# Later transposes by crossbar DMA, weights loaded behind them, PSUM banks given out by what was freed first, last output tile in two halves

## Chip, cores and metric

One core of one Trainium2 chip runs the whole program. The metric is the device time of one execution in microseconds; the lower the better. Executions of the kernel before lie within 0.6% of each other (238.12 to 239.59 us over all rounds), so a few tenths of a microsecond count only when the median of several runs, or the stage lengths of the traces, show them. "Span" is the part of an execution that the profile covers; the time of an execution is longer than its span by about two microseconds.

## The reference

A parallel transformer block in bf16: layernorm without weights, then sliding-window attention and a gated feed-forward, both from the same normalised rows, both added to the input.

```python
x: [1, 2048, 448]          # S = 2048, D = 448
xn = (x - mean) / sqrt(var + 1e-5)
q, k, v = split(xn @ wqkv) # H = 16 heads of Dh = 28
p  = softmax(mask(q @ k.T * Dh**-0.5))      # causal, window W = 256
a  = (p @ v) @ wo
b  = (gelu_tanh(xn @ w_gate) * (xn @ w_up)) @ w_down   # F = 1792
out = x + a + b
```

## The kernel before

It works in four blocks of 512 rows. Each block has an attention stage (twelve steps: four head groups of three steps, each with scores, an exponential on ScalarE, masks on GpSimd; after each group the product PV of the masked exponentials with V) and a gated feed-forward stage. While ScalarE computes exponentials, TensorE gets other work as filler: the down projection of the block before (`gen_down`) and the projections of the block after (`gen_proj`). The kernel uses eight PSUM banks; four hold the scores, the other four go by tags: `m` (two rotating), `d` and `o` (one each).

```python
    def transp(t, n, copy, tag):          # rows -> columns, on TensorE
        tp = psum.tile([P, 2, 4, P], bf16, name="tp", tag=tag, bufs=2 if tag == "m" else 1)
        for i in range(n):
            xn = xns.pop(t + i)
            for c in range(4):
                nc.tensor.transpose(out=tp[:, i, c, :], in_=xn[:, c, :], identity=ident[:, :])
        copy(out=xnT[:, :, t * P:(t + n) * P].rearrange("p c (i q) -> p i c q", q=P), in_=tp[:, 0:n, :, :])

    def gen_proj(qb):
        for t in (4 * qb, 4 * qb + 2):
            tag = ring[0][ring[1] % len(ring[0])]
            ring[1] += 1
            transp(t, 2, nc.vector.tensor_copy, tag)
            yield -830                    # nominal ns of filler
        yield from gen_v(qb, (4 * qb, 4 * qb + 2))
        yield from gen_qk(qb, range(4))

    def gen_down(qb, tags="odod"):        # one output tile of 128 rows at a time
        for tt in range(4):
            down_tag[0] = tags[tt]
            po = psum.tile([P, QB], f32, name="po", tag=tags[tt], ...)
            # 4 matmuls with wo, 14 with wd, yielding after every two        (cut)
            res = work.tile([P, D], bf16, name="res")
            nc.vector.tensor_tensor(out=res[:, :], in0=po[:, 0:D], in1=x_sb[:, t, :], op=ALU.add)
            nc.sync.dma_start(out=outv[:, t, :], in_=res[:, :])

    # gated(): up banks alternate between both m and both single ones
        turn = [0, 1] * 4
        # ... in begin(f)                                                 (cut)
            if f not in early:
                for tag, n in ((("m", 2), ("m", 2)), (("d", 1), ("o", 1)))[turn.pop(0)]:
                    pr["us"].append(psum.tile([P, QB], f32, name="u0", tag=tag, bufs=n))

    # attention(): PV takes the single bank that the current output tile does not hold
            ov = psum.tile([P, QB], f32, name="ov", tag="d" if down_tag[0] == "o" else "o", bufs=1)
```

## Time and profile before

| | before |
|---|---|
| time, median | 238.4 us (238.29 to 238.52; over all later rounds 238.12 to 239.59) |
| span of the profiled execution | 237.3 us (time of that execution 239.04) |
| first matmul of the V projection | 7.74 us |
| attention stages 1, 2, 3 (first `po` to first `u`) | 32.47, 32.51, 31.18 us |
| gated stages 1, 2, 3 (first `u` to first `po`) | 22.77, 22.77, 15.92 us |
| last addition starts | 231.73 us |

### The profile page before, as it was taken

To read this page: it belongs to the slowest core of one execution; us is meant where nothing else is said; L and a number is where in the kernel's file an instruction comes from. 1 tells how busy PE (TensorE), PEld (TensorE's weight loads), DVE (VectorE), ACT (ScalarE), POOL (GpSimd) and SP (SyncE) were. 2 spreads that over 40 slices of the span, in tenths; PEclk is the share of its full clock that TensorE was granted. 3 is DMA by queue.
4 is the path that set the end of the run, shared out by engine and by line. 5 is a ranking of instruction groups with operands and counts; after the bars stand their busy time and mean duration, and the time that the engine had idled before them with its cause. 6 is when DMAs were issued, how large, how long until landed. Compare 5 with 4: busy or idle time off the path is not lost.

```text
span 237.3 us, 4191 instructions
## 1 busy us (share of the span) xinstructions
PE 224.2 (94%) x1716; PEld 95.4 (40%) x1716; DVE 139.6 (59%) x283; ACT 135.2 (57%) x115; POOL 93.4 (39%) x116
## 2 busy tenths in 40 slices
PE   7799999999999999999999999999999899999990
PEld 2434333344544434344444434444344344333450
DVE  6897887769636666656634686464421865486211
ACT  4577798434967866322877768233587678363000
POOL 5024677220256877010075776220055867420000
PEclk9999999999999999999999999999999999999997
DMA  6999900000000000000000000000000000000010
GB/s 223 353 326 312 267 5 0 0 3 1 0 22 0 23 19 19 3 0 1 0 22 0 22 0 22 19 0 3 0 0 22 19 0 22 19 3 0 23 40 29
DMA packets 9010, 10.95 MB, mean 46 GB/s; under 512 B 600, under 2 KB 7960, under 8 KB 8984
## 3 DMA queue, kind: packets, MB, share of 16 engines
q1 hardware_dynamic: 8440, 9.81, 13.3%
q10 hardware_dynamic: 544, 0.80, 1.0%
q8 instruction: 15, 0.25, 0.5%
q14 instruction: 11, 0.09, 0.1%
HBM read 8.77 MB, written 1.84 MB: 45 GB/s over the span
## 4 chain that ended last, share of the span: by engine, by line
PE 78%; ACT 10%; DVE 4%; DMA 3%; issue 1%; POOL 1%; SPq 0%; ACTq 0%
PE gt L203 16%; PE po L288 16%; PE u L203 9%; ACT p_sb L450 7%; PE sc L446 6%; PE gt L208 5%; PE ov L420 4%; PE pq L203 4%; PE pk L203 4%; PE ue L203 4%; PE pv L203 3%; PE po L283 3%; DMA wv<-in_A_wqkv_dram 3%; PE pq L208 2%; ACT ge L357 2%; ACT L577 1%
## 5 line engine op out<-in xcount | busy, mean ns | idle before, releaser
L456 POOL TENSOR_SCALAR_AFFINE_SELECT p_sb<-p_sb 128x512 bf16<-128x512 bf16 (+1 forms) x92 | 69.6, 778 | 93.6 <-ACT p_sb L450 93.5
L450 ACT ACTIVATE p_sb<-sc 128x2048 bf16<-128x2048 f32 (+2 forms) x48 | 85.0, 1771 | 24.8 <-PE sc L446 20.6
L357 ACT ACTIVATE ge<-gt 128x1024 bf16<-128x1024 f32 x28 | 28.7, 1024 | 47.1 <-PE u L208 24.6
L288 PE MATMUL po<-wd,hT 128*128 128x448 bf16 x224 | 50.1, 353 | 0.0
L203 PE MATMUL gt<-xnT,wg 128*128 128x512 bf16 x168 | 40.5, 380 | 0.0
L361 DVE TENSOR_TENSOR hT<-ge,u 128x512 bf16<-128x512 bf16 x42 | 26.9, 683 | 18.4 <-ACT ge L357 18.3
L203 PE MATMUL u<-xnT,wu 128*128 128x512 bf16 x126 | 30.6, 379 | 0.6 <-DVE hT L322 0.6
L411 POOL TENSOR_TENSOR oN<-oc,rb 128x512 bf16<-128x512 f32 x16 | 21.0, 1314 | 23.8 <-DVE rb L405 23.8
L288 PEld LDWEIGHTS <-hT 128*128 128x128 bf16 x224 | 20.1, 98 | 20.5 <-issue 4.0
L424 DVE COPY oc<-ov 128x512 f32<-128x512 f32 x16 | 11.0, 690 | 22.2 <-PE ov L420 20.8
L203 PEld LDWEIGHTS <-wg 128*128 128x128 bf16 x168 | 15.1, 98 | 22.1 <-issue 6.0
L203 PEld LDWEIGHTS <-wu 128*128 128x128 bf16 x168 | 15.9, 98 | 20.0 <-issue 2.0
L446 PE MATMUL sc<-qT,kT 32*128 32x128 bf16 (+2 forms) x352 | 18.5, 275 | 1.6 <-ACT p_sb L450 1.1
L283 PE MATMUL po<-wo,oN 128*128 128x448 bf16 x64 | 15.9, 353 | 0.5 <-DVE hT L361 0.5
L293 DVE TENSOR_TENSOR res<-po,x_sb 128x448 bf16<-128x448 f32 x16 | 9.9, 616 | 10.1 <-PE po L288 10.0
L322 DVE CAST hT<-ue 128x512 bf16<-128x512 f32 x14 | 9.0, 683 | 11.1 <-PE ue L208 11.1
L420 PE MATMUL ov<-p_sb,v_sb 128*32 128x128 bf16 (+2 forms) x352 | 12.8, 277 | 1.5 <-POOL oN L411 0.8
L203 PE MATMUL pq<-xnT,wqp 128*128 128x512 bf16 (+1 forms) x51 | 13.3, 368 | 0.3 <-DVE v_sb L234 0.3
L208 PE MATMUL gt<-xnT,wgu 64*128 64x512 bf16 x49 | 13.3, 379 | 0.0
L203 PE MATMUL pk<-xnT,wkp 128*128 128x512 bf16 (+1 forms) x51 | 13.1, 366 | 0.1
L203 PE MATMUL pv<-wv,xnT 128*128 128x448 bf16 x48 | 11.1, 354 | 1.7 <-DMA wv<-in_A_wqkv_dram 1.4
L252 DVE CAST kT<-pk 128x512 bf16<-128x512 f32 (+1 forms) x17 | 10.9, 643 | 2.5 <-PE pk L208 2.5
(67 smaller groups left out, 206.0 us busy)
## 6 DMA issues: line engine op xcount, KB each, us to landing
out_dram<-res SPq DMA_DIRECT2D x16, 112.0 KB, 1.7
wd<-in_B_w_down_dram SPq DMA_DIRECT2D x1, 1568.0 KB, 12.8
wu<-in_B_w_up_dram SPq DMA_DIRECT2D x1, 1344.0 KB
wg<-in_B_w_gate_dram SPq DMA_DIRECT2D x1, 1344.0 KB, 14.5
x_sb<-in_A_x_dram SPq DMA_DIRECT2D x1, 896.0 KB
wraw<-in_A_wqkv_dram ACTq DMA_DIRECT2D x1, 672.0 KB
x_sb<-in_A_x_dram SPq DMA_DIRECT2D x1, 448.0 KB
wo<-in_A_wo_dram SPq DMA_DIRECT2D x4, 98.0 KB
```

The costliest lines, as they stand in the source:

```text
L203: nc.tensor.matmul(ps, lhsT=lhs(c), rhs=rhs(c), start=start and c == 0, stop=stop and c == 2, skip_group_check=True)
L208: nc.tensor.matmul(ps, lhsT=lhs[p0:p0 + 64], rhs=rhs[p0:p0 + 64], start=start, stop=stop, tile_position=(p0, 0), skip_group_check=True)
L283: nc.tensor.matmul(po[:, 0:D], lhsT=oN[:, g, cs], rhs=wo[:, g, :], start=(g == 0), stop=False, skip_group_check=True)
L288: nc.tensor.matmul(po[:, 0:D], lhsT=hT[:, f, cs], rhs=wd[:, f, :], start=False, stop=(f == NF - 1), skip_group_check=True)
L357: nc.scalar.activation(out=ge[:, :, :], in_=pr["gt"][:, :, :], func=ACT.Gelu_apprx_tanh)
L361: nc.vector.tensor_tensor(out=hT[:, f + i, :], in0=ge[:, i, :], in1=u[:, :], op=ALU.mult)
L411: nc.gpsimd.tensor_tensor(out=oN[:, g, :], in0=oc[:, :], in1=rb[:, :, :].rearrange("p a b -> p (a b)"), op=ALU.mult)
L420: nc.tensor.matmul(ov[32 * j:32 * j + 32, q0:q0 + nq], lhsT=v_sb[:, kt, h, :], rhs=p_sb[:, j, col:col + nq], start=(n == 0 and i == 0), st ...
L424: nc.vector.tensor_copy(out=oc[:, :], in_=ov[:, :])
L446: nc.tensor.matmul(ss[:, j, col:col + nq], lhsT=kT[r, g, kt * P:(kt + 1) * P], rhs=qT[r, g, qb * QB + q0:qb * QB + q0 + nq], start=True, s ...
L450: nc.scalar.activation(out=p_sb[:, :, 0:ncol], in_=ss[:, :, 0:ncol], func=ACT.Exp, scale=SCALE)
L456: nc.gpsimd.affine_select(out=reg, in_=reg, pattern=mid + [[1 if diag else -1, P]], compare_op=ALU.is_ge, fill=0.0, base=0 if diag else -1 ...
```

## The change

Four things, all to take TensorE work or TensorE waits away. (1) Tiles 4 to 15 are transposed by crossbar DMA (`dma_start_transpose`, a transfer that writes the tile transposed), and the weights, which would stand ahead of them in the same queue, are issued behind the first four (`loads`, called once tiles 6 and 7 are normalised in block 0). (2) The banks for up projections, output tiles and PV are chosen with the aim that the one freed first is used first. (3) In blocks 1 and 2 one pair of up projections moves from the gated stage into attention as filler, and the filler is shared out differently (`late`, `fresh`). (4) The last output tile is computed, added and stored in two halves.

```diff
+    def dma_transp(t):
+        nc.sync.dma_start_transpose(out=xnT[:, :, t * P:(t + 1) * P], in_=xns.pop(t)[:, :, :].rearrange("p a b -> p (a b)"))
 ...
     def gen_proj(qb):
-        for t in (4 * qb, 4 * qb + 2):
-            tag = ring[0][ring[1] % len(ring[0])]
-            ring[1] += 1
-            transp(t, 2, nc.vector.tensor_copy, tag)
-            yield -830
 ...
-    def gen_down(qb, tags="odod"):
+    def gen_down(qb, tags):
+            for n, (lo, up) in enumerate(((0, D),) if t < NT - 1 else ((0, D // 2), (D // 2, D))):
+                    if g % 2:
+                        fresh[0] = g == 1
 ...
-        turn = [0, 1] * 4
+        turn = [down_tag[0], "o" if down_tag[0] == "d" else "d"] * 4
 ...
+                alone = (turn.pop(0), 1)
+                tags = (("m", 2), alone)
+                if qb == 0 and f == 0:
+                    nxt = [ring[0][(ring[1] + i) % 3] for i in range(2)]
 ...
-                    share(feeds, whole / (left + 0.2) - ahead - to, to)
+                    late = 400 if i == 0 else 0
+                    share(feeds, (whole - late) / (left + 0.2) + late - ahead - to, to)
+                    if n == 0 and g and fresh[0]:
+                        feeds[0].run()
 ...
+    def loads():
+        for t in range(4, 8):
+            dma_transp(t)
+        nc.sync.dma_start(out=wu[:, :, :], in_=rows(B_w_up, 0, 3))
+        # ... the half rows, wg, wo, wd                                   (cut)
 ...
-            feeds = [Feed((gen_down(qb - 1), DOWN))]
+            tags = "dodo" if last_tag[0] == "o" else "odod"
+            feeds = [Feed((gen_down(qb - 1, tags), DOWN))]
-                plan = {0: 830, 1: 830, 2: 1140, 4: 1140, 5: 1300, 7: 1300, 8: 1300, 10: 1300}
+                new_hT(qb)
+                early = (2,)
+                feeds[1].gens.append(gen_up(qb, early))
+                feeds[1].left += UP1
+                plan = {0: 1140, 2: 1140, 4: 1300, 5: 1300, 7: 1300, 8: 1300, 10: 1300}
 ...
-    feed = Feed((gen_down(NB - 1, "dmom"), DOWN))
+    feed = Feed((gen_down(NB - 1, "dmomd" if last_tag[0] == "o" else "omdmo"), DOWN))
```

More of the change, by code (lines that the diff above doesn't have):

```diff
@@ L139 @@
     nc.sync.dma_start(out=x_sb[:, 8:16, :], in_=xv[:, 8:16, :])
-    nc.sync.dma_start(out=wu[:, :, :], in_=rows(B_w_up, 0, 3))
-    for t3, lo, hi in ((wgu3, B_w_gate, B_w_up), (wug3, B_w_up, B_w_gate)):
-        nc.sync.dma_start(out=t3[0:64, :], in_=lo[384:448, :])
-        nc.sync.dma_start(out=t3[64:128, :], in_=hi[384:448, :])
-    nc.sync.dma_start(out=wg[:, :, :], in_=rows(B_w_gate, 0, 3))
     eps_t = const.tile([P, 1], f32, name="eps_t")
@@ L257, in gen_proj @@
     def gen_proj(qb):
-        for t in (4 * qb, 4 * qb + 2):
-            tag = ring[0][ring[1] % len(ring[0])]
-            ring[1] += 1
-            transp(t, 2, nc.vector.tensor_copy, tag)
-            yield -830
         yield from gen_v(qb, (4 * qb, 4 * qb + 2))
         yield from gen_qk(qb, range(4))
-    PROJ, QK1 = 2 * 830 + 2 * 1500 + 4 * 1660, 1660
+    PROJ, QK1 = 2 * 1500 + 4 * 1660, 1660
     DOWN = 4 * 3400
@@ L271 @@
     hTs, oNs = {}, {}
-    down_tag = ["d"]
-    def gen_down(qb, tags="odod"):
+    down_tag, last_tag, fresh = ["d"], [None], [False]
+    def gen_down(qb, tags):
         hT, oN = hTs[qb], oNs[qb]
@@ L279, in gen_down @@
             cs = slice(tt * P, (tt + 1) * P)
-            down_tag[0] = tags[tt]
-            po = psum.tile([P, QB], f32, name="po", tag=tags[tt], bufs=2 if tags[tt] == "m" else 1)
-            for g in range(4):
-                nc.tensor.matmul(po[:, 0:D], lhsT=oN[:, g, cs], rhs=wo[:, g, :], start=(g == 0), stop=False,
-                                 skip_group_check=True)
-                if g % 2:
-                    yield 380
-            for f in range(NF):
-                nc.tensor.matmul(po[:, 0:D], lhsT=hT[:, f, cs], rhs=wd[:, f, :], start=False, stop=(f == NF - 1),
-                                 skip_group_check=True)
-                if f % 2 and f < NF - 1:
-                    yield 375
-            res = work.tile([P, D], bf16, name="res")
-            nc.vector.tensor_tensor(out=res[:, :], in0=po[:, 0:D], in1=x_sb[:, t, :], op=ALU.add)
-            nc.sync.dma_start(out=outv[:, t, :], in_=res[:, :])
-            yield 375
+            for n, (lo, up) in enumerate(((0, D),) if t < NT - 1 else ((0, D // 2), (D // 2, D))):
+                w = up - lo
+                tag = tags[tt + n]
+                down_tag[0] = tag
+                po = psum.tile([P, QB], f32, name="po", tag=tag, bufs=2 if tag == "m" else 1)
+                for g in range(4):
+                    nc.tensor.matmul(po[:, 0:w], lhsT=oN[:, g, cs], rhs=wo[:, g, lo:up], start=(g == 0), stop=False,
+                                     skip_group_check=True)
+                    if g % 2:
+                        fresh[0] = g == 1
+                        yield 380 * w // D
+                fresh[0] = False
+                for f in range(NF):
+                    nc.tensor.matmul(po[:, 0:w], lhsT=hT[:, f, cs], rhs=wd[:, f, lo:up], start=False, stop=(f == NF - 1),
+                                     skip_group_check=True)
+                    if f % 2 and f < NF - 1:
+                        yield 375 * w // D
+                res = work.tile([P, D], bf16, name="res")
+                nc.vector.tensor_tensor(out=res[:, 0:w], in0=po[:, 0:w], in1=x_sb[:, t, lo:up], op=ALU.add)
+                nc.sync.dma_start(out=outv[:, t, lo:up], in_=res[:, 0:w])
+                yield 375 * w // D
     def new_hT(qb):
@@ L328, in gated @@
         hT = hTs[qb]
-        turn = [0, 1] * 4
+        turn = [down_tag[0], "o" if down_tag[0] == "d" else "d"] * 4
         def begin(f):
+            last_tag[0] = turn[0] if f not in early else last_tag[0]
             pr = dict(f=f, gt=phase[0].pool.tile([P, 2, QB], f32, name="gt", tag="s"), us=[])
             if f not in early:
-                for tag, n in ((("m", 2), ("m", 2)), (("d", 1), ("o", 1)))[turn.pop(0)]:
+                alone = (turn.pop(0), 1)
+                tags = (("m", 2), alone)
+                if qb == 0 and f == 0:
+                    nxt = [ring[0][(ring[1] + i) % 3] for i in range(2)]
+                    tags = [(x, 2 if x == "m" else 1) for x in nxt]
+                for tag, n in tags:
                     pr["us"].append(psum.tile([P, QB], f32, name="u0", tag=tag, bufs=n))
@@ L529 @@
     norm(5)
-    wo_v = A_wo.rearrange("(g j d) n -> j d g n", g=4, j=4)
-    for j in range(4):
-        nc.sync.dma_start(out=wo[32 * j:32 * j + Dh, :, :], in_=wo_v[j])
-    nc.sync.dma_start(out=wd[:, :, :], in_=B_w_down.rearrange("(k p) n -> p k n", p=P))
     stat(7)
+    def loads():
+        for t in range(4, 8):
+            dma_transp(t)
+        nc.sync.dma_start(out=wu[:, :, :], in_=rows(B_w_up, 0, 3))
+        for t3, lo, hi in ((wgu3, B_w_gate, B_w_up), (wug3, B_w_up, B_w_gate)):
+            nc.sync.dma_start(out=t3[0:64, :], in_=lo[384:448, :])
+            nc.sync.dma_start(out=t3[64:128, :], in_=hi[384:448, :])
+        nc.sync.dma_start(out=wg[:, :, :], in_=rows(B_w_gate, 0, 3))
+        wo_v = A_wo.rearrange("(g j d) n -> j d g n", g=4, j=4)
+        for j in range(4):
+            nc.sync.dma_start(out=wo[32 * j:32 * j + Dh, :, :], in_=wo_v[j])
+        nc.sync.dma_start(out=wd[:, :, :], in_=B_w_down.rearrange("(k p) n -> p k n", p=P))
     for qb in range(NB):
@@ L539 @@
         if qb < 2:
-            aux = [lambda: rstd(6, 2), lambda: (norm(6), norm(7)), lambda: None] * (1 - qb) + [lambda t=t: stat(t) for t in range(8, 12)] * (1 - qb) + [lambda: rstd(4 * qb + 8, 4)]
+            aux = [lambda: rstd(6, 2), lambda: (norm(6), norm(7), loads()), lambda: None] * (1 - qb) + [lambda t=t: stat(t) for t in range(8, 12)] * (1 - qb) + [lambda: rstd(4 * qb + 8, 4)]
         if qb == 0:
@@ L571, in hook @@
                     norm(t + 2)
+                    dma_transp(t + 2)
                     if qb == 0:
```

## The prediction

> **What bounds the kernel now.** I read the page first, then the chain of work that ended last, TensorE's own waits, a table of busy time by stage, and last the timeline around each TensorE pause.
>
> ```profile
> PE 224.2 (94%) x1716; PEld 95.4 (40%) x1716; DVE 139.6 (59%) x283; ACT 135.2 (57%) x115; POOL 93.4 (39%) x116
> PE   7799999999999999999999999999999899999990
> PEclk9999999999999999999999999999999999999997
> PE 78%; ACT 10%; DVE 4%; DMA 3%; issue 1%; POOL 1%; SPq 0%; ACTq 0%
> ```
>
> TensorE is busy in every slice, at full clock, and makes 78% of the chain. The other engines are under 60%. So a microsecond of TensorE work removed should be nearly a microsecond won, unless another engine sets the pace of that stage. The stage table (start:end, length, then TensorE busy first) shows where one nearly does:
>
> ```profile
> 17.00:40.50 23.50, 22.43 (x196) 8.97 (x195) 18.22 (x38) 19.30 (x22) 14.96 (x21) 1.00 0.53 156
> 60.10:92.50 32.40, 31.78 (x305) 14.05 (x304) 19.32 (x36) 24.65 (x16) 20.18 (x25) 1.00 0.04 12
> 92.50:115.30 22.80, 22.80 (x138) 9.36 (x136) 13.02 (x27) 7.93 (x8) 3.28 (x4) 1.00 0.02 6
> 170.60:201.80 31.20, 29.90 (x282) 12.75 (x281) 16.05 (x30) 24.00 (x14) 19.85 (x25) 1.00 0.04 12
> ```
>
> The blocks alternate between an attention stage and a gated feed-forward stage. The gated stage is solid TensorE. The attention stage has twelve steps, and one score buffer, so scores and exponentials alternate: 1.88 us of ScalarE plus 0.56 us until the next scores. That is 2.44 us a step, or 29.3 us for twelve. Attention 1 runs from its first scores at 60.56 to the gated stage's first matmul at 92.56: 32.0 us. Summing its TensorE work by starts gives 30.2 us (scores 4.0, PV 2.3, transposes 0.9, V projection 2.9, QK 6.6, down projection 72 x 0.1885 = 13.6). Add some 0.9 us of switches between tile shapes and 0.9 us of true waits. TensorE is therefore still the bound there, with ScalarE's floor 2.7 us below it.
>
> The waits that the change can reach, from the timeline (start, length, what; the bracket is the idle time ahead and what ended it):
>
> ```profile
> 20.96 1.07 PE L198 MATMUL tp<-ident,xn 128*128 128x128 bf16 x16
> 22.37 1.31 PE L203 MATMUL pv<-wv,xnT 128*128 128x448 bf16 x6 [0.34 <-DVE xnT L199]
> 40.51 1.46 PE L203 MATMUL u<-xnT,wu 128*128 128x512 bf16 x6 [0.56 <-DVE hT L322]
> 63.26 0.40 PE L446 MATMUL sc<-qT,kT 32*128 32x384 bf16 x8 [0.23 <-ACT p_sb L450]
> 86.34 0.84 PE L420 MATMUL ov<-p_sb,v_sb 128*32 128x128 bf16 x24 [0.34 <-DVE res L293]
> 217.71 0.92 PE L283 MATMUL po<-wo,oN 128*128 128x448 bf16 x4 [0.54 <-DVE hT L361]
> 231.73 0.62 DVE L293 TENSOR_TENSOR res<-po,x_sb 128x448 bf16<-128x448 f32 x1 [2.78 <-PE po L288]
> ```
>
> Each of the middle four is TensorE waiting for a PSUM bank or the score buffer. The last is the tail: an addition of 0.62 us with TensorE finished, then 4.95 us to the end of the span.
>
> **What the Trainium skill says.** "TensorE: Matmul & The Clock Gate", Part 4, gives about 275 to 390 ns for a 128x128 bf16 transpose on TensorE. The trace's records say 219 ns each, but eight start to finish their issue in 0.45 us (61.66 to 62.11), 56 ns each; I count 56 ns. This is what "Perfetto Trace Analysis", Identifying the Most-Contended Engine, warns of: matmul busy time is a bad distance to the roofline, because matmuls are pipelined. I use starts for that reason. Its Matmuls section asks that groups rotate through PSUM banks so that evacuation overlaps; the waits at 40.51, 86.34 and 217.71 are where this kernel's rotation picks a bank freed last. "Advanced Engine Details and Errata", X-Bar Transpose (TRN2), expects 350 to 400 GB/s of a crossbar transpose. For one tile of 128 x 512 x 2 bytes = 131 KB that is an estimate of 0.35 us; no transposing DMA is in this trace. The landing latency I take from the plain output stores, 1.7 us for 112 KB, and allow 2 to 4 us in all.
>
> **The change part by part.**
>
> *Transposes.* Tiles 4 to 15 leave TensorE: 48 transposes, 48 x 56 ns = 2.7 us, in six groups of 0.45 us, and six DVE copies of 0.69 us, beside other work. In block 0 the wait for the copy goes too: 20.96 to 22.37 is 1.41 us, of which I take 1.25, because the score buffer then frees a little later than TensorE wants it. For tiles 4 and 5 the normalised rows are ready at 15.5 us and wanted at 21. For 6 and 7 they are ready at 18.75 and wanted at about 23.5, a margin of 4.7 us for two transfers. For tiles 8 to 15 the normalisation is in the gated stage before, and wanted 2 us or more after its end.
>
> *Weights behind them.* wu, the four half rows, wg, wo and wd are 1344 + 896 + 1344 + 392 + 1568 KB = 5.68 MB. The first 17 us moved 303 GB/s, so they take about 18.7 us. Started at about 21 us they end near 40. wu is in by 26 (first used near 33.5), wg by about 33 (used at 40), wd by 40 (used at 59). So no cost, with 7 us to spare.
>
> *One up pair moves.* In blocks 1 and 2 one pair of up projections moves into attention as filler: six matmuls of 0.2155 us, a half pair of 0.32 and a switch, +1.7 us there. The gated stage loses 1.3 + 0.2 = 1.5 us. Attention 1: 32.0 - 0.9 (transposes) + 1.7 - 0.23 (step 0 gets 0.4 us more filler, so that the wait at 63.26 goes) - 0.38 (two more matmuls are put ahead of the PV whose bank was just read, 86.34) = 32.2. With the gated stage at -1.5 and perhaps +0.2, because its second up bank is now the one of the last output tile (its addition ends at 93.38, wanted at 93.21), block 1 is -1.1 us. Block 2 has the same pattern (waits of 0.28 at 118.55 and 0.34 at 141.62): -1.2.
>
> *Banks.* Block 0's first up pair takes the banks next in the ring: the u matmul moves from 40.51 to about 39.9, -0.6. The final down projection starts in a bank freed long before: last u matmul at 216.79 plus 0.21, so 217.05 in place of 217.71, -0.65. In attention 3 the scores wait 0.35 us in step 0, and a PV waits 0.82 us for a bank; I count half of that sum as won, less a possible new bank wait of 0.3: -0.4.
>
> *Tail.* The last addition handles 224 columns in place of 448: 448 / 0.96 per ns is 0.47 of the 0.62 us, so half of 0.47 is won, 0.23. The extra 18 matmuls have half the columns, 0.093 us each; transposes issue at 56 ns with their weight loads, so loads do not bind. -0.25.
>
> Sum: -1.25 - 0.6 (block 0) - 1.1 - 1.2 - 0.4 - 0.65 - 0.25 = -5.45 us. 238.4 - 5.45 = 232.95 us.
>
> **The rivals.**
>
> *The crossbar is slow or its issue is.* If each transpose holds the issuing queue 3 us instead of at most 1, tiles 6 and 7 would land near 27 to 28, not 22.5, and V of those tiles would wait some 4 us in block 0; the weights would slide too, into the use of wu. Against it: the data is only 0.13 MB each and the rings are empty from about 12 us, since the x and QKV loads are some 3 MB. Time then: 236 to 238.
>
> *ScalarE takes over in attention.* For it: the floor is 29.3 us, and removed TensorE work in steps 0 and 1, which already run at 2.43 us, wins nothing there. Against it: the moved up pair refills exactly what the transposes leave, and other steps are above the floor (81.59 to 84.51 is 2.92 us, 84.51 to 87.64 is 3.13). If it did hold, blocks 1 and 2 would give nothing in attention but still their 1.5 us each in the gated stage, so the sum hardly moves; in block 3, where no transpose is removed and most steps are at 2.45, it would leave 0 instead of -0.4.
>
> *New bank waits.* One bank of two single ones now serves every up pair of the gated stage, together with one of the rotating pair. Reuse distance is two pairs as before, so I expect no wait inside. At the seam the addition of the last output tile stands behind DVE's transposes (202.34 in block 3), so the wait could be 0.5 us three times, 1 us more than I count: 234.
>
> *More is won.* Fewer DVE copies shorten other waits, and attention 3 gives up its full 1.2 us: 231.5.
>
> **Range and chances.** The transposes and the two seam banks are nearly sure, 3.8 us with the six groups; the rest hangs on orders of tenths of a microsecond. The first rival gets about one chance in eight. That gives 232.9, with 230.8 to 235.6 eight times in ten. The 2% line is 238.4 x 0.98 = 233.6, only 0.7 us above my number: faster 0.62, same 0.36, slower 0.02.
>
> **What would show it.** Right: TensorE has no tp groups after 10 us; pv of tiles 4 and 5 starts near 21 us and that of 6 and 7 has no DMA wait; u starts near 38.6 in block 0 (1.25 + 0.6 earlier); the gated stages of blocks 1 and 2 last about 21.4 us, and their attention stages keep about 32 us; the last po group follows the last u within 0.1 us; the last addition takes about 0.38 us. Wrong: TensorE waiting for xnT from a DMA, or for wu; attention stages above 33 us; a u wait on the output addition of over 0.3 us.

## More of the kernel before

Stage lengths are differences of starts on TensorE. They repeat to a few hundredths of a microsecond from trace to trace, so they show far smaller effects than the time does.

## The result and the profile after

235.12 us (234.3 to 235.73, four runs) against 238.46 (238.29 to 238.63): ratio 0.9858, 95% interval 0.9821 to 0.9895. That is 1.4% faster, inside "within 2%", and inside the predicted range, 2.2 us above the predicted 232.9. Ratios here and below are the mean time of one kernel's runs over the mean of the other's in the same rounds, so not quite the ratio of the medians quoted. Run twice more with five runs each, the changed kernel gave 0.9843 and 0.9854.

Busy time and the first line of the chain that ended last, from the page of the changed kernel:

```profile
PE 219.2 (94%) x1664; PEld 94.0 (40%) x1686; DVE 136.6 (59%) x280; ACT 135.0 (58%) x115; POOL 93.8 (40%) x116
PE 76%; DVE 8%; ACT 7%; issue 2%; DMA 2%; SPq 1%; POOL 1%; ACTq 0%
```

TensorE is 5.0 us less busy by the page and is still the chain. (Some 1.8 us of the 5.0 are no saving: this trace lacks 22 matmul records, 1664 against 1686 weight loads, and the gaps that they leave stand in the list of waits as 0.8 + 0.5 + 0.5 us of "issue".) But DVE's share of the chain doubled from 4% to 8%. That is the first hint of where gain was lost. The same four stages as in the prediction, in the changed kernel's own times (start:end, length, then TensorE busy first):

```profile
16.60:38.10 21.50, 21.21 (x178) 8.03 (x178) 16.31 (x35) 18.76 (x21) 14.33 (x20) 1.00 0.91 247
57.70:90.70 33.00, 32.16 (x294) 13.74 (x296) 18.89 (x37) 24.32 (x16) 19.76 (x25) 1.00 0.06 16
90.70:112.50 21.80, 21.23 (x128) 8.67 (x128) 12.59 (x26) 8.30 (x8) 3.99 (x4) 1.00 0.11 24
167.30:197.70 30.40, 29.32 (x277) 12.85 (x280) 16.25 (x30) 23.96 (x15) 19.76 (x25) 1.00 0.04 13
```

The gated stage was solid TensorE before; now 0.6 us of its 21.8 is idle: 0.36 us is the wait on an addition shown below, 0.16 us the gap of a missing record. The transposing DMAs, first as a row of the list of DMA issues (count, median us from issue to landing):

```profile
xnT<-xn SPq DMA_TRANSPOSE x12, 2.5
```

and in the list of what uses the tile `xn` (duration of the issue in ns, minimum/median/maximum, then the first and last start in us):

```profile
L189 SPq DMA_TRANSPOSE xnT<-xn x12: 1188/1190/2067, 14.6 to 112.5; - x12
```

The places that the prediction looked at, from the timeline of the changed kernel: V of tiles 4 and 5, the first up pair of block 0, the final output tiles, and the last addition:

```profile
20.57 1.31 PE L202 MATMUL pv<-wv,xnT 128*128 128x448 bf16 x6
38.13 1.47 PE L202 MATMUL u<-xnT,wu 128*128 128x512 bf16 x5
...
213.19 0.92 PE L280 MATMUL po<-wo,oN 128*128 128x448 bf16 x4
...
227.26 0.39 DVE L292 TENSOR_TENSOR res<-po,x_sb 128x224 bf16<-128x224 f32 x1 [1.33 <-PE po L287]
```

The predicted waits are gone from all of them. (A `x5` is a group of six with one matmul record missing from the trace.) TensorE's own waits show what came instead; columns are total us, times, longest:

```profile
PE u L202 <- DVE res L292: 0.7, 2, 0.4
PE ov L425 <- POOL oN L416: 0.4, 1, 0.4
PE ov L425 <- DVE res L292: 0.4, 1, 0.4
```

`res` is the addition that reads a finished output tile out of its PSUM bank. The timeline of DVE and TensorE at one PV of attention 1 shows the mechanism:

```profile
74.58 0.65 DVE L250 CAST qT<-pq 128x512 bf16<-128x512 f32 x1
74.67 0.92 PE L280 MATMUL po<-wo,oN 128*128 128x448 bf16 x4
75.15 0.67 DVE L251 CAST kT<-pk 128x512 bf16<-128x512 f32 x1
75.43 0.54 PE L287 MATMUL po<-wd,hT 128*128 128x448 bf16 x2
75.75 0.61 DVE L292 TENSOR_TENSOR res<-po,x_sb 128x448 bf16<-128x448 f32 x1
...
76.41 0.84 PE L425 MATMUL ov<-p_sb,v_sb 128*32 128x128 bf16 x24 [0.44 <-DVE res L292]
```

The old output tile is finished when the new one starts at 74.67. But DVE takes two casts first, and the addition starts only at 75.75, when the second is about done; so the bank is free only at 76.36 and PV starts at 76.41. The wait put down to POOL in the list is the same thing in attention 2: there the addition ended at 131.16 and PV started at 131.21. GpSimd's multiplication (`oN`) and an exponential end within 0.01 us of that too, so these moments alone do not tell which of the three it was. Other PVs do: at 184.42 in the same trace PV starts 0.84 us before both of those end, and in none of the 14 traces does a PV start while an addition runs or less than 0.05 us after it. And at the start of the gated stage:

```profile
91.28 0.58 DVE L292 TENSOR_TENSOR res<-po,x_sb 128x448 bf16<-128x448 f32 x1
91.92 0.81 PE L202 MATMUL u<-xnT,wu 128*128 128x512 bf16 x3 [0.36 <-DVE res L292]
```

The first of the two up groups starts at 90.75 and would be done at 91.40 (three matmuls of 0.2155 us). The second now sits in the bank of the last output tile and starts at 91.92: 0.52 us lost. Some 0.2 us of it would be lost even to an addition that starts at once; b4 below, where no DVE transpose is ahead of it, takes 1.69 us for the six matmuls in place of 1.46. The other 0.3 us are the wait behind a 0.71 us transpose on DVE, which ran from 90.64.

### The profile page after: what moved, and what is told of

It is laid out like the page before. It is cut to its first block, busy times and chain, and to the rows that moved or that the text cites. A ratio compares the mean times of both kernels' runs of the same rounds, so it can differ in the third digit from the quotient of the medians.

```text
span 232.3 us, 4132 instructions
## 1 busy us (share of the span) xinstructions
PE 219.2 (94%) x1664; PEld 94.0 (40%) x1686; DVE 136.6 (59%) x280; ACT 135.0 (58%) x115; POOL 93.8 (40%) x116
## 4 chain that ended last, share of the span: by engine, by line
PE 76%; DVE 8%; ACT 7%; issue 2%; DMA 2%; SPq 1%; POOL 1%; ACTq 0%
PE gt L202 16%; PE po L287 15%; PE u L202 10%; ACT p_sb L455 6%; PE sc L451 6%; PE gt L207 5%; PE ue L202 5%; PE ov L425 4%; PE po L280 4%; PE pq L202 3%; PE pk L202 3%; PE pv L202 2%; DMA wraw<-in_A_wqkv_dram 2%; PE pq L207 2%; DVE res L292 1%
## 5 line engine op out<-in xcount | busy, mean ns | idle before, releaser
L287 PE MATMUL po<-wd,hT 128*128 128x448 bf16 (+1 forms) x238 | 50.5, 342 | 0.0
L366 DVE TENSOR_TENSOR hT<-ge,u 128x512 bf16<-128x512 bf16 x38 | 24.3, 682 | 16.8 <-ACT ge L362 16.7
L287 PEld LDWEIGHTS <-hT 128*128 128x128 bf16 x238 | 21.6, 98 | 20.1 <-issue 4.0
L202 PE MATMUL u<-xnT,wu 128*128 128x512 bf16 x109 | 27.4, 379 | 1.1 <-DVE res L292 0.7
L321 DVE CAST hT<-ue 128x512 bf16<-128x512 f32 x18 | 11.6, 684 | 14.2 <-PE ue L207 14.2
L292 DVE TENSOR_TENSOR res<-po,x_sb 128x448 bf16<-128x448 f32 (+1 forms) x17 | 9.9, 585 | 11.1 <-PE po L287 11.1
L280 PE MATMUL po<-wo,oN 128*128 128x448 bf16 (+1 forms) x68 | 15.7, 342 | 0.0
L425 PE MATMUL ov<-p_sb,v_sb 128*32 128x128 bf16 (+2 forms) x352 | 12.8, 277 | 0.9 <-POOL oN L416 0.4
L202 PE MATMUL pq<-xnT,wqp 128*128 128x512 bf16 (+1 forms) x44 | 12.4, 366 | 0.9 <-issue 0.5
L202 PE MATMUL ue<-xnT,wu 128*128 128x512 bf16 x48 | 12.0, 380 | 0.8 <-issue 0.8
L233 DVE CAST v_sb<-pv 128x448 bf16<-128x448 f32 x12 | 7.1, 617 | 9.6 <-PE pv L207 9.6
```

The source lines that it names most:

```text
L202: nc.tensor.matmul(ps, lhsT=lhs(c), rhs=rhs(c), start=start and c == 0, stop=stop and c == 2, skip_group_check=True)
L280: nc.tensor.matmul(po[:, 0:w], lhsT=oN[:, g, cs], rhs=wo[:, g, lo:up], start=(g == 0), stop=False, skip_group_check=True)
L287: nc.tensor.matmul(po[:, 0:w], lhsT=hT[:, f, cs], rhs=wd[:, f, lo:up], start=False, stop=(f == NF - 1), skip_group_check=True)
L292: nc.vector.tensor_tensor(out=res[:, 0:w], in0=po[:, 0:w], in1=x_sb[:, t, lo:up], op=ALU.add)
L366: nc.vector.tensor_tensor(out=hT[:, f + i, :], in0=ge[:, i, :], in1=u[:, :], op=ALU.mult)
L425: nc.tensor.matmul(ov[32 * j:32 * j + 32, q0:q0 + nq], lhsT=v_sb[:, kt, h, :], rhs=p_sb[:, j, col:col + nq], start=(n == 0 and i == 0), st ...
```

## The experiments

Three batches, each on one chip with the kernel before in the same rounds. All results were correct.

| run | what it is | median us | ratio to before (95%) | time less span, mean us |
|---|---|---|---|---|
| a1_after_again | changed | 234.95 | 0.9843 (0.9828 to 0.9858) | 2.35 |
| a2_dma_only | before, with DMA transposes alone | 235.54 | 0.9881 (0.9864 to 0.9899) | 1.79 |
| a3_pe_transp | changed, transposes on TensorE | 237.57 | 0.9954 (0.9939 to 0.997) | 1.78 |
| a4_bank_swap | changed, other single bank first | 233.71 | 0.9797 (0.9779 to 0.9815) | 2.32 |
| b1_swap_no_tail | a4, last tile whole | 233.53 | 0.9769 (0.9751 to 0.9787) | 1.78 |
| b2_fresh4_no_tail | b1, more filler ahead of PV | 233.54 | 0.9783 (0.9766 to 0.98) | 1.73 |
| b3_loads_early | changed, weights ahead of transposes | 247.3 | 1.035 (1.0329 to 1.0371) | 2.15 |
| b4_early_off | changed, no up pair moved | 234.63 | 0.9821 (0.9804 to 0.9838) | 2.51 |
| c1_after_third | changed | 234.96 | 0.9854 (0.9831 to 0.9877) | 2.44 |
| c2_no_tail | changed, last tile whole | 234.65 | 0.9828 (0.9806 to 0.985) | 1.80 |
| c3_one_store | changed, halves but one store | 235.35 | 0.9845 (0.983 to 0.986) | 2.14 |
| c4_best | a4's swap, no moved pair, whole tile | 233.23 | 0.9763 (0.9748 to 0.9779) | 1.78 |

The kernel before has medians of 238.44, 238.83 and 238.84 us in the three batches, and time less span of 1.77, 1.74 and 1.80.

Stage lengths from the profiled execution of each, as differences of starts on TensorE (block 0 is first `pv` to first `po` of attention 1; attention is first `po` to first `u`; gated is first `u` to first `po`; the last column is first `po` of the final output tiles to the start of the last addition):

| run | block 0 | att. 1 | gated 1 | att. 2 | gated 2 | att. 3 | gated 3 | last tiles |
|---|---|---|---|---|---|---|---|---|
| before | 52.35 | 32.47 | 22.77 | 32.51 | 22.77 | 31.18 | 15.92 | 14.02 |
| changed | 50.37 | 33.02 | 21.78 | 33.02 | 21.78 | 30.41 | 15.45 | 14.07 |
| a2_dma_only | 50.37 | 31.91 | 22.78 | 31.95 | 22.77 | 31.19 | 15.91 | 14.02 |
| a3_pe_transp | 51.76 | 33.86 | 21.79 | 33.86 | 21.79 | 30.41 | 15.44 | 14.07 |
| a4_bank_swap | 50.37 | 33.01 | 21.27 | 33.02 | 21.26 | 30.41 | 15.22 | 14.06 |
| b2_fresh4_no_tail | 50.37 | 32.99 | 21.26 | 32.99 | 21.26 | 30.56 | 15.22 | 14.02 |
| b4_early_off | 50.38 | 31.37 | 23.00 | 31.38 | 23.00 | 30.42 | 15.44 | 14.07 |
| c4_best | 50.37 | 31.58 | 22.56 | 31.59 | 22.55 | 30.41 | 15.21 | 14.03 |

**a1_after_again**: no edit.

> The changed kernel again, to see whether its times really scatter (234.3 to 235.7 us so far, against 238.3 to 238.6 for the kernel before) and how the span of the trace goes with the time. Theory 'steady gain': 234.3 to 235.7 again, the span 232.2 to 233.3, no TensorE wait on a DMA after 10 us. Theory 'late transposes': in the longer runs V of tiles 6 and 7 waits for the crossbar, up to 1 us.

It came to 234.49 to 234.96 us. No wait on a crossbar transfer appears, neither here nor in the profile of c3 (235.65 us, the slowest execution with this order of loads that was profiled), so "late transposes" falls as far as profiles go; the executions up to 236.13 us were not profiled. The spread between 234.3 and 235.7 of the first runs goes with the span (232.2 to 233.3). A part of it may be the first V matmul, which waits for its weights and starts anywhere from 7.22 to 7.76 us in the profiled executions of all kernels. The kernel before was profiled in an execution where it started late (7.74), which no part of the change accounts for.

**a2_dma_only**: the kernel before, with part (1) alone.

```diff
# against the kernel before
+        nc.sync.dma_start_transpose(...)       # tiles 4 to 15
-            transp(t, 2, nc.vector.tensor_copy, tag)
+    def loads(): ...                           # weights behind the first four
-                plan = {0: 830, 1: 830, 2: 1140, 4: 1140, 5: 1300, 7: 1300, 8: 1300, 10: 1300}
+                plan = {2: 1140, 4: 1140, 5: 1300, 7: 1300, 8: 1300, 10: 1300}
```

> The kernel before with only the transposes of tiles 4 to 15 moved to the crossbar and the weights behind them; banks, up pair, sharing of filler and tail as before. Theory 'TensorE time': six groups of 0.45 us go and the wait for the copy in block 0, so 2 to 3.2 us off, about 235.5 to 236.4. Rival 'ScalarE floor': in blocks 1 and 2 the removed work lay in steps that already run at 2.44 us, so only block 0 gains, 1.2 us off, 237.2.

235.54 us: 2.9 us off, as "TensorE time" has it. The floor is refuted: attention 1 and 2 gave up 0.56 us each. Block 0 gained 1.98 us. It includes the 0.6 us of the up pair's bank wait, although this kernel has the old choice of bank. The transposes took two of the places that are dealt out in turn from the ring `m`, `m`, `d`. Without them the filler pair ahead of the gated stage falls on `m` and `d` in place of both `m`, as counting the draws in the code shows, and the wait is gone from the trace. Attention gained less than the 0.9 us of transposes: one PV's wait for an addition, 0.34 us in the kernel before (86.34), grew to 0.82, with a cast ahead of the addition, in attention 1 at

```profile
82.86 0.61 DVE L287 TENSOR_TENSOR res<-po,x_sb 128x448 bf16<-128x448 f32 x1
...
83.52 0.84 PE L414 MATMUL ov<-p_sb,v_sb 128*32 128x128 bf16 x24 [0.82 <-POOL oN L405]
```

(The bracket names GpSimd, which again ends at the same moment, 83.47.)

**a3_pe_transp**: the changed kernel without part (1).

```diff
# against the changed kernel
+            transp(t, 2, nc.vector.tensor_copy, tag)
-                    dma_transp(t + 2)
+    nc.sync.dma_start(out=wu[:, :, :], in_=rows(B_w_up, 0, 3))    # and the other weights, early as before
-                plan = {0: 1140, 2: 1140, ...
+                plan = {0: 830, 1: 1970, 2: 1140, ...
```

> The changed kernel with the transposes back on TensorE and the weights loaded early, all else as changed. Theory 'TensorE time': this loses what a2 gains, 2 to 3.2 us above the changed kernel, so about 237 to 238. If banks, filler and tail were worth what I predicted for them (2.3 us net of new waits), it is 236 or less.

237.57 us, 2.6 us above the changed kernel (a1, same batch). So the transposes are worth 2.6 to 2.9 of the whole gain of 3.5 us, and banks, filler and halves together are worth only 0.9 us (ratio 0.9954), not the 2.3 predicted. (The plan of filler in a3 is of neither kernel, so a better plan might give a little more.) The two parts do not simply add: the 0.6 us of block 0 is in both.

**a4_bank_swap**: give the first up pair the single bank that the last output tile does not hold, and the last PV the other one.

```diff
         hT = hTs[qb]
+        if qb:
+            down_tag[0] = "o" if down_tag[0] == "d" else "d"
         turn = [down_tag[0], "o" if down_tag[0] == "d" else "d"] * 4
```

> The changed kernel with one thing different: in blocks 1 to 3 the first up pair's second bank is the single bank that the last output tile does not hold, and the last PV takes the other. Theory 'new bank wait': the waits of 0.4 to 0.5 us on the output addition at the start of gated stages 1 to 3 go, so 1.0 to 1.3 us off the changed kernel. Rival: the wait only moves to the PV or the first exponential, and the time stays within 0.3 us.

233.71 us, 1.24 us below a1. Gated 1, 2 and 3 became 0.51, 0.52 and 0.23 us shorter, together 1.26 us, and nothing grew. The six up matmuls at the start of gated 1 now run as one group, with no wait inside:

```profile
91.12 1.46 PE L202 MATMUL u<-xnT,wu 128*128 128x512 bf16 x6
```

**b1_swap_no_tail**: a4 with the last tile whole.

```diff
-            for n, (lo, up) in enumerate(((0, D),) if t < NT - 1 else ((0, D // 2), (D // 2, D))):
+            for n, (lo, up) in enumerate(((0, D),) if True else ()):
```

> The bank swap of a4, with the last output tile whole again. In the traces so far the time is 1.8 us longer than the span where the tile is whole, or the transposes are on TensorE, and 2.3 us where both parts of the change are in. Theory 'the halves win 0.25': the time is 0.2 to 0.3 us above a4 (ratio 0.9797), near 0.981. Rival 'the halves cost outside the span': the span grows by 0.25 us but the time less the span falls to 1.8, so the time is 0.2 to 0.4 us below a4, near 0.978.

The time less the span fell to 1.78 as the rival said, and the ratio to 0.9769. The intervals of b1 and a4 still touch and the chips differ, so c2 repeats it.

**b2_fresh4_no_tail**: b1, with filler ahead of PV until four pairs of matmuls of the new output tile are out.

```diff
-                        fresh[0] = g == 1
+                        fresh[0] = True
-                fresh[0] = False
+                    fresh[0] = f < 3
-                    if n == 0 and g and fresh[0]:
+                    while n == 0 and g and fresh[0] and feeds[0].gens:
                         feeds[0].run()
```

> b1 with one thing more: ahead of a PV, filler runs until four pairs of matmuls of the new output tile are out, not two, so that the output addition has time to free the bank even behind two casts on DVE (a PV waits 0.4 us for it in attention 1 and 2). Theory 'a PV still waits for the addition': 0.5 to 0.9 us below b1. Rival: the scores come later and ScalarE's floor takes it back, within 0.2 us of b1.

233.54 against 233.53 us: nothing won, and the rival holds. The waits on the addition are gone from the list of TensorE's waits, and this stands there in their place:

```profile
PE sc L453 <- ACT p_sb L457: 1.7, 5, 0.3
```

In b1 that row is 0.6 us in two waits. The first of those PVs starts 18.69 us after the first `po` in both kernels: the filler filled the wait and did not shorten it. And filler is a fixed amount. Used ahead of a PV, it is missing in a later step, where TensorE then waits for ScalarE. Attention 1 is 32.99 in place of 33.02.

**b3_loads_early**: the weights where the kernel before loads them.

```diff
+    nc.sync.dma_start(out=wu[:, :, :], in_=rows(B_w_up, 0, 3))    # and the rest, right after x
     def loads():
         for t in range(4, 8):
             dma_transp(t)
-        nc.sync.dma_start(out=wu[:, :, :], in_=rows(B_w_up, 0, 3))
-        ...
```

> The changed kernel with the weights loaded where the kernel before loads them, ahead of the transposes on the same queue. Theory 'in order behind the loads': the four transposes of block 0 land only when 5.7 MB have gone, near 30 us, and V of block 1's tiles waits 6 to 9 us: 240 to 243. Rival 'transposes pass': small transfers share the rings and land 3 us after issue, time within 0.5 us of the changed kernel.

247.3 us, worse than even the theory said. TensorE stood still for 11.39 us:

```profile
31.90 2.42 PE L208 MATMUL pv<-wv,xnT 128*128 128x448 bf16 x6 [11.39 <-DMA xnT<-xn]
```

```profile
PEclk9999559999999999999999999999999999999999
```

```profile
L195 SPq DMA_TRANSPOSE xnT<-xn x12: 1188/1196/8305, 19.5 to 126.0; - x12
DMA to landing us min/median/max: 2.4/3.7/12.4
```

The first is from the timeline of b3, the second is its granted clock in 40 slices, from the page, the third is what its transposes took. wo's issue keeps the queue from 11.34 to 17.9 us, and the first transpose then keeps it for 8.3 us, from 19.45, and lands 12.4 us after it began, when wd, issued just before it, has landed too (18.48 + 12.8 us). That is "in order behind the loads". During the pause the granted clock falls to half, at 23.5 us, 3.0 us after the last matmul, and stays there until 37.1 us (six V matmuls take 2.42 us, not 1.31): the part that the expectation did not have. So "weights behind them" is not a refinement but what makes the crossbar usable here: some 12 us between the two orders (247.3 against 234.95 in a1).

**b4_early_off**: no up pair moved in blocks 1 and 2.

```diff
-                new_hT(qb)
-                early = (2,)
-                feeds[1].gens.append(gen_up(qb, early))
-                feeds[1].left += UP1
-                plan = {0: 1140, 2: 1140, 4: 1300, 5: 1300, 7: 1300, 8: 1300, 10: 1300}
+                plan = {0: 1140, 2: 1140, 4: 1300, 5: 1300, 7: 1300, 8: 1300}
```

> The changed kernel without the up pair moved into attention in blocks 1 and 2. Theory 'TensorE time is only moved': attention gets 1.7 us shorter as far as ScalarE's floor of 29.3 lets it, the gated stage 1.5 longer; 0 to 0.6 us slower than the changed kernel. Rival 'the pair is what makes the transposes pay': ScalarE's floor holds attention at its old length, and the time is 2 us or more above the changed kernel.

Neither: 234.63 us, ratio 0.9821, not slower than the changed kernel (0.9843 and 0.9854 on other chips; the intervals of 0.9821 and 0.9843 touch). The stages say it more sharply. Attention 1 plus gated 1 is 54.37 us here, 54.80 in the changed kernel, 55.24 before. Attention falls to 31.37, well above ScalarE's 29.3, so no floor holds it. The moved pair takes 1.2 us off the gated stage and adds 1.65 to attention, 0.44 of them the PV's wait, which is not in b4's trace.

**c1_after_third**: no edit; the base of its batch.

> The changed kernel as the base of this batch, on the same chip as the next three: 234.3 to 235.7 us, ratio 0.983 to 0.986, time less span 2.3 us.

234.96 us; one run of 236.13 lies above the expected range.

**c2_no_tail**: the changed kernel with the last tile whole (the edit of b1).

> The changed kernel with the last output tile whole, nothing else. Theory 'the halves cost': the time is 0.2 to 0.6 us below c1 and the time less the span is 1.75. Prediction's term: 0.25 us above c1. Also the time from the end of the last addition to the end of the execution, 6.3 to 6.9 us so far for whole tiles against 7.0 to 7.6 with halves, should fall by about 0.5.

The means are 235.24 (c1) and 234.72 (c2): 0.5 us below, 0.3 by the medians. The sign is that of "the halves cost"; the 95% intervals overlap, so by time alone it is not clear. What is clear is where it goes: the time less span is 1.68 to 1.90 us in every run of every kernel with a whole last tile, and 2.10 to 2.78 in every run of the changed kernel, a4 and b4, which have halves and DMA transposes. Working out the time from the end of the last addition to the end of the profiled execution gives 6.28 to 6.90 us for the six kernels with a whole tile (mean 6.69) and 6.96 to 7.61 for the six profiles with halves, b3 and c3 left out (mean 7.20; those two give 6.93 and 7.69). The halves shorten the addition from 0.62 to 0.39 us, cost 0.05 us of matmuls, and lengthen what comes after by half a microsecond in the mean, with a scatter as large as that within each group.

**c3_one_store**: two halves computed and added, one store.

```diff
-                res = work.tile([P, D], bf16, name="res")
-                nc.vector.tensor_tensor(out=res[:, 0:w], in0=po[:, 0:w], in1=x_sb[:, t, lo:up], op=ALU.add)
-                nc.sync.dma_start(out=outv[:, t, lo:up], in_=res[:, 0:w])
+                if n == 0:
+                    res = work.tile([P, D], bf16, name="res")
+                nc.vector.tensor_tensor(out=res[:, lo:up], in0=po[:, 0:w], in1=x_sb[:, t, lo:up], op=ALU.add)
+                if up == D:
+                    nc.sync.dma_start(out=outv[:, t, :], in_=res[:, :])
```

> The changed kernel with the last tile computed and added in two halves, but stored by one DMA. Theory 'the extra store or its short rows cost': time less span back to 1.75, 0.4 to 0.8 us below c1, and below c2 by the 0.2 us of the shorter addition. Rival 'the halves themselves (bank, extra matmuls)': as c1.

235.35 us, mean equal to c1's, time less span 2.14. The extra store and its 448-byte rows are not what costs, or not alone. What the halves do after the last store stays open: the profile has no instruction there, and a3, with halves but transposes on TensorE, has the ordinary 1.78 outside the span and its long end (5.47 us after the addition) inside it.

**c4_best**: a4's swap, b4's and b1's edits together.

> The bank swap, no up pair moved and the last tile whole. Theory 'waits for the output addition are what the moved pair costs': 1.2 to 2.0 us below c1, ratio 0.975 to 0.978, no TensorE wait on the addition. Rival: 0.5 us or less below c1.

233.23 us, 1.7 us below c1 (2.1 by the means), ratio 0.9763: 2.4% faster than the kernel before and clear of the changed one (0.9854, interval 0.9831 to 0.9877). No wait on the addition is left. It is level with b1 (0.9769), so with the swap the moved pair costs little: 54.28 us (a4) against 54.14 for attention 1 plus gated 1. Swap and whole tile are what matters.

## Why the prediction was right and where it was not

The time lies in the range, and "TensorE is the bound, what is removed from it is won" held for the transposes (2.6 to 2.9 us) and the waits at the seams, the places where one stage or output tile follows another (1.2 us in a4). It did not hold for the PV waits that b2 removed. The most probable outcome, faster by over 2%, did not come. That the range held is in part luck: two of the first four executions (235.61 and 235.73) lie above its end of 235.6. One of the prediction's own signs of being wrong came, a wait of `u` on the addition of over 0.3 us (0.36); attention 1, counted as there from its first scores, took 32.55 us, between the 32 expected and the 33 that would have been a sign. Term by term, predicted against the stage table (profile before against profile after):

| term | predicted | measured |
|---|---|---|
| block 0: transposes, copy wait, ring banks | -1.85 | -1.98 |
| block 1 | -1.1 | +0.55 - 0.99 = -0.44 |
| block 2 | -1.2 | +0.51 - 0.99 = -0.48 |
| attention 3 | -0.4 | -0.77 |
| last down projection's first bank | -0.65 | gated 3 is -0.47, with 0.23 of new wait in it (a4) |
| tail: matmuls and shorter addition | -0.25 | +0.05 - 0.23 = -0.18 |
| after the last addition | 0 | about +0.5 to +0.7 |
| sum | -5.45 | -4.32 up to the last addition, about -3.6 to -3.8 in all |

The upper end of the last term comes from c1 less c2: 0.52 + 0.18 = 0.70 us; the lower one from the means of the profiled executions. -4.32 + 0.7 = -3.6 is what the means of a1 and c1 show (-3.70 and -3.60; c1 stands on both sides, so only a1 is a check).

**Block 0** was right in size, though not in its split: a2 shows that the bank wait goes with the transposes alone, a3 that the bank choice alone also removes it. The crossbar's landing (2.4 to 3.1 us) fell within the 2 to 4 allowed, and its issue, 1.19 us, was slightly over the "at most 1" of the first rival, with enough margin. (A side sum of the prediction, 3.8 us, cannot be rebuilt: 2.7 us of transposes and the two seam banks, 0.6 and 0.65, make 3.95.)

**Blocks 1 and 2** are the step that failed: 1.38 us of the missing 1.9 or so. The prediction counted -0.23 and -0.38 us for waits that `late` and `fresh` remove, and "perhaps +0.2" for the up pair's new bank. The waits at those places did go. But the extra filler moved the seam between two output tiles, and another PV of the same stage fell just behind a seam: +0.44 us at 76.41, which no term had. And the new bank cost 0.52 us, not 0.2, because I took the addition to start as early as before (0.2 us after the last matmul), while in this order it stands behind a DVE transpose. The third rival had said 0.5 us at the seams and 234; that one should have been the main line. Counting the start of gated 3, a4 took back 1.26 us of it. The PV wait cannot be had the same way: b2 removed it and got nothing.

**Attention 3** gave twice its term. The PV wait of 0.82 us at 188.58 in the kernel before is gone in full, and the new bank wait that was set against it did not come; the score wait of 0.35 stayed (0.33).

**The tail** most likely failed in sign: c2 is 0.5 us below c1 in the mean and b1 is below a4, though neither pair is clear by time alone. Up to the addition the term was right, 0.62 less 0.39 us being the 0.23 predicted. But the sum ended at the last addition and assumed that whatever follows is the same in both kernels. It is not, by about half a microsecond in the mean, and c3 speaks against the simplest cause, the second store. The cause stays open.

**ScalarE as the next bound** did not take over as a floor of the stage: a2 and b4 shortened attention by 0.56 and 1.10 us. It acts locally, as b2 shows: where the filler had been used ahead of a PV, later steps waited for an exponential (1.7 us in five waits).

## What to carry to other kernels

When filler is moved between stages that alternate two engines, look at what frees each bank, and at what stands ahead of that reader in its own engine's queue; here a bank "freed first" in program order was not free first where a cast or a transpose was ahead of its reader. Put bulk loads behind small urgent transfers on the same queue, and take the order of a queue as part of the change. Judge a change at the end of a kernel by the time of the execution and not by the last visible instruction.

## What the Trainium skill lacked or had wrong

- "DMA: Bandwidth & Descriptors", Rules for kernel authors: a transpose next to ordinary DMAs "needs nothing". That is about correctness. For the time it did not hold here: ordinary loads ahead of the transposes in the same queue cost some 12 us (247.3 us in b3, 234.95 for the changed kernel), with one TensorE wait of 11.39. The rule could say so.
- "Advanced Engine Details and Errata", X-Bar Transpose (TRN2), gives a bandwidth of 350 to 400 GB/s and, in that section, no latency. (Elsewhere the skill has a time for one 128x128 block; what I miss is one for a tile of four such blocks.) Twelve transposes of 131 KB, SBUF to SBUF, took 1.19 us each to issue (median) and 2.5 us from issue to landing; worked out, that is 52 GB/s for one that is waited for.
- "TensorE: Matmul & The Clock Gate", Part 4, gives about 275 to 390 ns per transpose. That is the duration of one (219 ns in this trace); eight in a row took 0.45 us by their starts, 56 ns each, in a kernel that keeps TensorE busy, and a saving has to be counted by the latter. The same page's closing table asks for no pauses above some 3 us between matmul bursts; b3 agrees, with the granted clock at half 3.0 us into a pause of 11.39 us and six V matmuls at 2.42 us after it, against 1.31.
- No page that I found has it that the time outside the profiled span depends on the kernel (where the skill speaks of time outside a kernel, it gives fixed figures): 1.74 to 1.80 us for the kernel before, 2.35 and 2.44 for the changed one, 1.80 with the last tile whole.
